# Gram inputs in 4 KB rows, own PSUM banks for the first Gram blocks, VectorE copying part of them, and raw weights queued directly behind the first loads

## The chip, the cores and the metric

The kernel runs on one core of a Trainium2 chip. The metric is the device time of one execution in microseconds (us); lower is better. The core has a matrix engine (TensorE, PE in the profile, with PEld for its weight loads), VectorE (DVE), ScalarE (ACT), GpSimd (POOL) and SyncE (SP), whose instruction stream issues all DMA transfers of this kernel.

## What is computed

A delta-rule attention runs over 768 steps for 4 x 8 heads of width 48; its output, 3072 tokens of 384 features, passes through two dense layers with a hidden width of 2048 each.

```
k_n = k / (norm(k) + 1e-6)
for t in range(S):
    y[:, :, t] = einsum('bhd,bhde->bhe', q[:, :, t], state)
    v_old = einsum('bhde,bhd->bhe', state, k_n[:, :, t])
    state += beta[t] * einsum('bhd,bhe->bhde', k_n[:, :, t], v[:, :, t] - v_old)
x  = y as (3072, 384)
x1 = elu(x @ w_in) @ w_out
h  = x1 @ w_in2
g  = (a0 + a1 h + a2 h^2 + a3 h^3) / (1 + |b0| |h| + |b1| h^2 + 1e-6)
out = g @ w_out2
```

## The kernel before, in words

**Attention.** The 768 steps are cut into 12 sub-chunks `s` of 64 steps, and two sub-chunks make one of six windows `w` (512 tokens over the four batches). For each sub-chunk, `g_item` builds Gram blocks (k times [k, q]) in two steps, `bb` = 0 and 1, of 64 small matmuls each into two PSUM tiles (`gp`, one for each `hf`). From each tile VectorE writes the masked k-q part to `p`; ScalarE copies two 32-column diagonal pieces to `gd` and one off-diagonal piece to `lo`. When the four Gram steps of a window are done, VectorE turns `gd` over into `am` (`pre1`) and works through a triangular inverse of about 60 dependent small operations (`row`, `merge`), whose last step turns the result into `tp_t` (`post`). Then `chain` runs the sub-chunks one after the other: solve (`cb`), lower part (`lo`), second solve, outputs (`y`, turned over as `xt`), state update (`ku` into `s_bd`), and for s > 0 the product with the state (`ks`).

**Dense layers.** For each window the first layer takes 16 steps `H` (hidden block `h`) and `O` (output block `o`), each nine matmuls of 128x512. The second layer follows for six groups of 512 tokens. Operands are split in a high and a low part. The weights come as 8-byte numbers: `conv_load` brings a 192 KB piece into one of eight slots inside the tile `wo1` (shown as `wo` in the trace), and `conv_x` (two ScalarE operations), `conv_d` (VectorE: three or two SCALAR_TENSOR_TENSOR operations of 128x192 a piece, written to `wo` and `ce`) and `conv_s` turn it into the high and low part, `wi` for the first matrix.

**Order.** Every operation is first recorded by `Recorder` with the dependencies that its tiles make. `order` then lays out the five engines' streams from these dependencies and from tables of durations and switching costs (`PEC`, `LEAVE`, `PAIR`, `SLACK`), with pseudo-random tie-breaks from the seeds in `MIX`. Two engines that read one PSUM tile are put one behind the other in the order in which the program names them. Before the first wide matmul, `gaps` puts `fill` matmuls (128x256, no result used) into planned idle time of TensorE; each runs as two passes in the trace.

**Around the change.** Gram inputs are loaded by `gin_ahead`, once for each sub-chunk and `bb`: two transfers of 48 partitions (rows 0 to 47 and 64 to 111), each with two 2 KB pieces a partition. The first six tiles are parked in buffers that are not needed yet (`wo1`, then `xs`, `xh`, `xl`; the trace shows `wo` and `xg`); later ones use two rotating buffers `gin`, and each Gram step frees its tile and asks for the next. Gram PSUM tiles come from the pool `pa` of three banks. `start` issues the first loads; `chain_loads` follows with `kq`, `kv` and the first eight pieces of raw weights.

Of the kernel before, what the change touches and what calls it, by code (L numbers as in the profile page):

```python
# [20 lines left out]
D = 48  # L21
# [8 lines left out]
HD = DM // 2  # L30
NV = 7
Q = dict(
# [142 lines left out]
class Recorder:  # L175
    def __init__(self, nc):
        self.nc, self.ops, self.group, self.live = nc, [], None, False

# [80 lines left out]
    def dma(self, out, in_):  # L259
        v = out if isinstance(out, View) else in_  # L260
        n = v.ids.size * 4 * (v.part[1] - v.part[0])
        self.add("SP", self.nc.sync.dma_start, dict(out=out, in_=in_), [out], [in_], SLACK["issue"], 2000, n)

# [45 lines left out]
LEAVE = {"F": 2040, "so": 774, "lo": 812, "ks": 960, "gp": 970, "ku": 855, "yy": 1471, "xx": 290, "wm": 500, "yt": 1400}  # L309
ENTER = {"F": 0, "so": 71, "ks": 71, "xx": -25, "ku": 70, "yy": 20, "gp": 60, "lo": 100, "wm": 50, "yt": 20}  # L310
PAIR = {
# [3 lines left out]
SIZE = {"F": 9, "yy": 16, "yt": 48}  # L315
SLACK = {"small": 150, "F": 100, "x": 30, "issue": 560, "rate": 240, "land": 2300, "wait": 1500, "space": 3900, "room": 290, "first": 432, "hold": 400, "jit": 300, "pj": 0}
MIX = [
    (1076044, 1), (92414181, 200), (90150106, 200), (77610261, 20), (97147800, 60), (84287398, 200),
    (75730493, 60), (8425654, 600),
]  # L320
# [241 lines left out]
def kernel(  # L562
# [172 lines left out]
    gin_t = {}  # L735
    gin_q = [(w, j, s, bb) for w in range(NW) for j, s in enumerate(WINS[w]) for bb in range(2)]
    gin_n = [0]
# [11 lines left out]
    def gin_ahead(n):  # L749
        for _ in range(n):  # L750
            i = gin_n[0]
            if i == len(gin_q):
                return
            park = i < 6
            if park or gin_l[0] < 2:
                w, j, s, bb = gin_q[i]
# [5 lines left out]
                t = t.rearrange("p (f n) -> p f n", f=2)  # L762
# [36 lines left out]
    def g_item(j, s, bb):  # L799
# [6 lines left out]
        t, n = gin_t.pop((s, bb))  # L806
        for i in range(4):
            for blk in range(2):
                for hf in range(2):
                    for h in range(2):  # L810
                        rows, c = slice(64 * h, 64 * h + D), 128 * i
                        mm(out=ps[hf][grp(hf, h, blk), i], lhsT=t[rows, hf, c + 32 * blk:c + 32 * blk + 32], rhs=t[rows, hf, c:c + 128],
                           start=True, stop=True)
        gin_l[0] -= n
        gin_ahead(1)
        for hf in range(2):
            u0, v0 = 16 * j + 8 * hf + 4 * bb, 8 * hf + 4 * bb
            vector.tensor_tensor(
                out=p_t[:, v0:v0 + 4], in0=ps[hf][:, :, 64:128],
                in1=mp_sb[hf].unsqueeze(1).to_broadcast([128, 4, 64]), op=ALU.mult)  # L820
            b0, b1 = halves(hf)
            act(out=gd[b0, u0:u0 + 4], in_=ps[hf][b0, :, 0:32], func=AF.Copy)
            act(out=gd[b1, u0:u0 + 4], in_=ps[hf][b1, :, 32:64], func=AF.Copy)
            act(out=lo_t[b0, 4 * bb:4 * bb + 4], in_=ps[hf][b0, :, 32:64], func=AF.Copy)
# [513 lines left out]
    def start():  # L1338
        gpsimd.memset(gd, 0.0)
        gpsimd.memset(s_bd, 0.0)  # L1340
        gin_ahead(1)
        rc.dma(out=cm_sb, in_=mask_p)
        gin_ahead(NV)
        load_beta(0)
        rc.dma(out=mh_sb, in_=mask_h)

    def chain_loads():
        for nm in ("kq", "kv"):
            for _ in range(2 if nm == "kq" else 2):
                ch_ahead(nm)  # L1350
        conv_ahead()

    def coefs():
# [204 lines left out]
```

## Time and profile before

| | |
|---|---|
| median of 3 runs | 1002.14 us (1002.08 to 1002.99) |
| the profiled execution | 1002.51 us, of which the span of its instructions is 1000.7 us |
| TensorE / VectorE / ScalarE / GpSimd busy | 98% / 85% / 75% / 38% of the span |
| DMA | 96.77 MB, mean 97 GB/s |

A span starts with the first instruction and ends with the last; 1.81 us of the profiled execution lie outside it. The share of busy time is a mean over stages that have different limits, so the stages are shown apart below.

### The profile page before, as it was taken

To read this page: it belongs to the slowest core of one execution; us is meant where nothing else is said; L and a number is where in the kernel's file an instruction comes from. 1 tells how busy PE (TensorE), PEld (TensorE's weight loads), DVE (VectorE), ACT (ScalarE), POOL (GpSimd) and SP (SyncE) were. 2 spreads that over 40 slices of the span, in tenths; PEclk is the share of its full clock that TensorE was granted. 3 is DMA by queue.
4 is the path that set the end of the run, shared out by engine and by line. 5 is a ranking of instruction groups with operands and counts; after the bars stand their busy time and mean duration, and the time that the engine had idled before them with its cause. 6 is when DMAs were issued, how large, how long until landed. Compare 5 with 4: busy or idle time off the path is not lost.

```text
span 1000.7 us, 25423 instructions
## 1 busy us (share of the span) xinstructions
PE 982.7 (98%) x10402; PEld 801.3 (80%) x10402; DVE 846.6 (85%) x1218; ACT 753.1 (75%) x1524; POOL 382.5 (38%) x282
## 2 busy tenths in 40 slices
PE   6999999999999999999999999999999999999997
PEld 4877878877887887788888888888888888888885
DVE  3999969987995998799666477889999999999996
ACT  3779799887877887887788778676676676766763
POOL 2353546542331242223222244364363643633332
PEclk9999999999999999999999999999999999999998
DMA  9554074226426432641545932001010010000000
GB/s 236 141 166 156 20 216 140 64 82 209 139 66 184 146 115 77 183 139 64 163 121 187 357 125 79 1 23 42 0 64 1 1 64 1 32 1 0 32 1 31
DMA packets 61588, 96.77 MB, mean 97 GB/s; under 512 B 7072, under 2 KB 39968, under 8 KB 61472
## 3 DMA queue, kind: packets, MB, share of 16 engines
q1 hardware_dynamic: 61472, 95.15, 30.4%
q8 instruction: 81, 1.33, 0.6%
q14 instruction: 35, 0.29, 0.1%
HBM read 73.11 MB, written 22.02 MB: 95 GB/s over the span
## 4 chain that ended last, share of the span: by engine, by line
PE 95%; DVE 2%; ACT 1%; issue 1%; DMA 0%; SPq 0%; ACTq 0%; DVEq 0%
PE o L193 39%; PE h L193 19%; PE h_b L193 10%; PE h_a L193 9%; PE fill L1478 4%; PE cb L193 3%; PE y L193 3%; PE gp L193 3%; PE ku L193 1%; PE ks L193 1%; PE h_c L193 1%; PE xt L193 1%; ACT wo L193 1%; DVE wo L193 1%; DMA wo<-c_kq 0%
## 5 line engine op out<-in xcount | busy, mean ns | idle before, releaser
L193 POOL TENSOR_TENSOR wor<-wo,wor 128x384 fp32r<-128x384 f32 x96 | 114.9, 1199 | 283.9 <-ACT wor L193 260.3
L193 POOL TENSOR_TENSOR gl<-wo 128x1024 fp32r<-128x1024 f32 x47 | 138.8, 2953 | 189.1 <-DVE wo L193 142.8
L193 PE MATMUL o<-gh,wor 128*128 128x512 f32 x576 | 195.1, 396 | 0.0
L193 PE MATMUL h<-xh,wi 128*128 128x512 f32 x546 | 185.5, 398 | 0.0
L193 ACT ACTIVATE wo<-wo 128x1024 f32<-128x1024 f32 (+3 forms) x224 | 142.3, 672 | 41.9 <-DVE wo L193 37.8
L193 PE MATMUL o<-gh,wo 128*128 128x512 f32 x576 | 139.7, 391 | 0.0
L193 PEld LDWEIGHTS o<-gh,wor 128*128 128x128 f32 x576 | 108.1, 188 | 23.9 <-issue 0.2
L193 PEld LDWEIGHTS o<-gh,wo 128*128 128x128 f32 x576 | 108.9, 189 | 22.7
L193 PEld LDWEIGHTS h<-xh,wi 128*128 128x128 f32 x546 | 102.4, 188 | 23.1 <-issue 0.6
L193 PE MATMUL o<-gl,wor 128*128 128x512 f32 x288 | 112.2, 390 | 0.0
L193 PE MATMUL h<-xl,wi 128*128 128x512 f32 x273 | 106.4, 390 | 0.3 <-DVE xl L193 0.3
L193 DVE SCALAR_TENSOR_TENSOR e<-e,pe 128x512 f32<-128x512 f32 x96 | 74.4, 775 | 37.4 <-ACT e L193 36.6
L193 DVE SCALAR_TENSOR_TENSOR wo<-wo 128x192 int32<-128x192 int32 (+2 forms) x101 | 87.4, 869 | 17.9 <-ACT wo L193 17.6
L193 PE MATMUL h_b<-xh,wi 128*128 128x512 f32 x300 | 96.4, 389 | 0.0
L193 DVE TENSOR_TENSOR gl<-e,gh 128x512 fp32r<-128x512 f32 x88 | 74.1, 843 | 20.2 <-ACT gh L193 19.9
L193 PE MATMUL h_a<-xh,wi 128*128 128x512 f32 x276 | 88.9, 389 | 0.0
L193 ACT ACTIVATE wo<-h_b,ab_sb 128x1024 f32<-128x1024 f32 (+1 forms) x52 | 57.3, 1128 | 33.5 <-PE h_b L193 33.5
L193 PE MATMUL o<-gl,wo 128*128 128x512 f32 x288 | 73.8, 391 | 2.0 <-DVE gl L193 2.0
L193 ACT ACTIVATE e<-h 128x512 f32<-128x512 f32 x91 | 54.4, 597 | 27.1 <-PE h L193 25.8
L193 DVE SCALAR_TENSOR_TENSOR gh<-wo,ab_sb 128x1024 fp32r<-128x1024 f32 (+1 forms) x49 | 63.3, 1293 | 7.5 <-ACT wo L193 1.7
L193 ACT ACTIVATE wo<-h_a,ab_sb 128x1024 f32<-128x1024 f32 x46 | 52.0, 1161 | 21.2 <-PE h_a L193 19.7
L193 ACT ACTIVATE wor<-wo 128x384 fp32r<-128x384 f32 x96 | 50.3, 524 | 21.6 <-PE o L193 19.6
(125 smaller groups left out, 2037.8 us busy)
## 6 DMA issues: line engine op xcount, KB each, us to landing
kq<-c_kq SPq DMA_DIRECT2D x22, 512.0 KB, 4.5
kv<-c_kv SPq DMA_DIRECT2D x24, 384.0 KB, 4.7
raw<-w_out SPq DMA_DIRECT2D x42, 192.0 KB, 2.7
gin<-c_kq SPq DMA_DIRECT2D x36, 192.0 KB, 3.8
raw<-w_in SPq DMA_DIRECT2D x34, 192.0 KB, 2.9
o2d<-cs SPq DMA_DIRECT2D x32, 192.0 KB, 2.5
i2d<-cs SPq DMA_DIRECT2D x32, 192.0 KB, 2.7
wi<-i2d SPq DMA_DIRECT2D x16, 384.0 KB, 3.3
```

Source lines behind the costliest of these rows:

```text
L193: fn(**{k: v.real() if isinstance(v, View) else v for k, v in kw.items()})
L1478: nc.tensor.matmul(out=wt["w"][:, 0:256], lhsT=c[:, 128:256], rhs=c, start=True, stop=True)
```

## The change

Gram inputs are loaded once for each sub-chunk and `hf`, 112 partitions of one 4 KB row in a single transfer (448 KB, with the 16 empty rows between the two blocks of 48); both tiles of a sub-chunk serve both Gram steps and come free after the second. The second Gram step of all uses the two PSUM tiles of the first dense layer (`h0`, `h1`), the third two of its output tiles (`o1`, `o2`). In the first window VectorE copies the `gd` pieces of `hf` = 1. Eight pieces of raw weights are queued behind the fourth Gram load, and all later transfers are put behind them until `chain_loads` has been recorded. The planner's tables and seeds change too.

```
-    wm1=6, wk=4, wr=3, wr0=4)
+    wm1=6, wk=4, wr=3, wr0=4, wl=8, gh=1)
...
+        if v.ids.size >= 1024:
+            n *= .75
+        o = self.add("SP", self.nc.sync.dma_start, dict(out=out, in_=in_), [out], [in_], SLACK["issue"], 2000, n)
+        if self.behind is not None:
+            o.deps.setdefault(self.behind, "s")
+        self.sent = o
...
-    "F": (226.7, 425), "gp": (27.3, 475), "ks": (13.4, 330), "so": (22, 220), "lo": (22, 250), "yy": (85, 262), "ku": (47, 263),
+    "F": (226.7, 425), "gp": (29, 475), "ks": (18, 330), "so": (22, 220), "lo": (22, 250), "yy": (85, 262), "ku": (47, 263),
...
-                for h in range(2):
-                    rows = slice(64 * h, 64 * h + D)
-                    rc.dma(out=t[rows], in_=c_kq[s, :, rows, 4 * bb:4 * bb + 4, :].rearrange("f p u n -> p f (u n)"))
-                gin_t[s, bb] = t, not park
+                t = t.rearrange("p (u n) -> p u n", u=8)
+                rc.dma(out=t[0:64 + D], in_=c_kq[s, hf, 0:64 + D])
+                gin_t[s, hf] = t, not park
...
-        ps = [pa.tile([128, 4, 128], F32, tag="pa", name="gp") for _ in range(2)]
+        i = 2 * s + bb
+        if i == 1:
+            ps = h_s
+        elif i == 2:
+            ps = [po.tile([128, 512], F32, tag=t, name="gp") for t in ("o1", "o2")]
+        else:
+            ps = [pa.tile([128, 512], F32, tag="pa", name="gp") for _ in range(2)]
...
-        gin_l[0] -= n
-        gin_ahead(1)
+        if bb:
+            for hf in range(2):
+                gin_l[0] -= gin_t.pop((s, hf))[1]
+            gin_ahead(2)
...
+            if j == s and hf == Q["gh"]:
+                vector.tensor_copy(out=gd[b0, u0:u0 + 4], in_=ps[hf][b0, :, 0:32])
+                vector.tensor_copy(out=gd[b1, u0:u0 + 4], in_=ps[hf][b1, :, 32:64])
+            else:
+                act(out=gd[b0, u0:u0 + 4], in_=ps[hf][b0, :, 0:32], func=AF.Copy)
+                act(out=gd[b1, u0:u0 + 4], in_=ps[hf][b1, :, 32:64], func=AF.Copy)
...
-        gin_ahead(NV)
+        gin_ahead(3)
         load_beta(0)
+        conv_loads(Q["wl"])
+        rc.behind = rc.sent
         rc.dma(out=mh_sb, in_=mask_h)
+        for _ in range(2):
+            ch_ahead("kv")
+        gin_ahead(4)
```

What the tables do to the streams shows in the streams themselves. In the rows a name before the arrow is written and the names behind it are read; `x8` counts equal rows.

SyncE's stream from the program's start, before (`wo_86` is the tile `wo1`, `bl` is beta, `cm_sb` the masks, `mh_sb` a small mask):

```order
1 L193 DMA wo_86<-c_kq 48x2x512 x2
2 L193 DMA cm_sb<-mask_p 128x256
3 L193 DMA wo_86<-c_kq 48x2x512 x4
4 L193 DMA xg<-c_kq 48x2x512 x2
5 L193 DMA bl<-beta_l 128x32
6 L193 DMA xg<-c_kq 48x2x512 x4
7 L193 DMA gin<-c_kq 48x2x512 x4
8 L193 DMA kv<-c_kv 128x768 x2
9 L193 DMA mh_sb<-mask_h 128x2
10 L193 DMA kq<-c_kq 128x1024 x2
11 L193 DMA wo_86<-w_in 128x384 x8
```

The same place of the stream with the change:

```order
1 L192 DMA wo_86<-c_kq 112x1024 x2
2 L192 DMA xg<-c_kq 112x1024
3 L192 DMA wo_86<-c_kq 112x1024
4 L192 DMA cm_sb<-mask_p 128x256
5 L192 DMA bl<-beta_l 128x32
6 L192 DMA wo_86<-w_in 128x384 x8
7 L192 DMA xg<-c_kq 112x1024 x2
8 L192 DMA gin<-c_kq 112x1024 x2
9 L192 DMA kv<-c_kv 128x768 x2
10 L192 DMA mh_sb<-mask_h 128x2
11 L192 DMA kq<-c_kq 128x1024 x2
12 L192 DMA raw<-w_out 128x384 x2
```

The raw weights move from behind sixteen Gram transfers, `kv` and `kq` to behind the four Gram transfers of the first window; the masks move from the third place to the fifth.

VectorE's stream at the program's start, before (the Gram blocks of the first window, the turn into `am`, and the first steps of the inverse):

```order
1 L193 TENSOR_TENSOR p<-gp,cm_sb 128x256 x8
2 L193 STREAM_TRANSPOSE am<-gd 128x1024
3 L193 TENSOR_TENSOR p<-gp,cm_sb 128x256
4 L193 TENSOR_SCALAR x<-am 128x32
5 L193 TENSOR_TENSOR p<-gp,cm_sb 128x256
6 L193 TENSOR_TENSOR nb<-rr,x 128x32
```

And with the change, from the third Gram step on (rows with `wo_86` and `ce` are weight conversions):

```order
6 L192 TENSOR_TENSOR p<-gp,cm_sb 128x256
7 L192 COPY gd<-gp 64x128 x2
8 L192 TENSOR_TENSOR p<-gp,cm_sb 128x256
9 L192 SCALAR_TENSOR_TENSOR wo_86<-wo_86 128x192
10 L192 TENSOR_TENSOR p<-gp,cm_sb 128x256
11 L192 COPY gd<-gp 64x128 x2
12 L192 TENSOR_TENSOR p<-gp,cm_sb 128x256
13 L192 STREAM_TRANSPOSE am<-gd 128x1024
14 L192 SCALAR_TENSOR_TENSOR wo_86<-wo_86 128x192
15 L192 TENSOR_SCALAR x<-am 128x32
16 L192 SCALAR_TENSOR_TENSOR ce<-wo_86 128x192 x2
17 L192 SCALAR_TENSOR_TENSOR wo_86<-wo_86 128x192 x2
```

Eight copies stand ahead of the turn, and conversions begin there. From the turn into `am` to the turn into `tp_t` the stream holds 22 conversions before and 35 with the change; from there to the first subtraction for the dense layer (`xl`) 30 and 28.

SyncE's stream beside the second window's dense layer, before:

```order
47 L193 DMA raw<-w_in 128x384 x2
48 L193 DMA gin<-c_kq 48x2x512 x2
49 L193 DMA kq<-c_kq 128x1024
50 L193 DMA wo_86<-w_out 128x384 x2
51 L193 DMA gin<-c_kq 48x2x512 x2
```

And with the change:

```order
45 L192 DMA raw<-w_out 128x384 x2
46 L192 DMA gin<-c_kq 112x1024 x2
47 L192 DMA kq<-c_kq 128x1024
48 L192 DMA wo_86<-w_in 128x384 x2
49 L192 DMA kv<-c_kv 128x768
```

The two Gram transfers there now bring the whole next sub-chunk into the two buffers that the step before has just freed. TensorE's stream has two groups of nine wide matmuls between that step and the next one, where it had one.

## Rows read from the trace of the kernel before

**Rows 1.** The page's first part: busy time, share of span and instructions of each engine.

```profile
PE 982.7 (98%) x10402; PEld 801.3 (80%) x10402; DVE 846.6 (85%) x1218; ACT 753.1 (75%) x1524; POOL 382.5 (38%) x282
```

**Rows 2.** Engines' busy time in four stretches; then granted clock, DMA share, GB/s.

```profile
0.00:19.05 19.05, 9.79 (x260) 6.61 (x260) 3.03 (x9) 6.69 (x24) 3.84 (x7) 1.00 0.96 187
19.05:57.40 38.35, 38.11 (x398) 32.26 (x398) 35.45 (x78) 26.28 (x97) 14.83 (x18) 1.00 0.58 181
57.40:88.10 30.70, 28.96 (x855) 22.80 (x853) 28.25 (x77) 25.93 (x83) 14.09 (x22) 1.00 0.60 187
88.10:1000.70 912.60, 905.79 (x8897) 739.59 (x8892) 779.86 (x1057) 694.24 (x1322) 349.73 (x235) 1.00 0.28 88
```

**Rows 3.** Waits of TensorE from 88 us on: total us, times, longest.

```profile
PE o L193 <- DVE gl L193: 2.0, 1, 2.0
PE h L193 <- DVE xl L193: 0.3, 1, 0.3
```

**Rows 4.** Timeline of TensorE: start, duration, operation, count, wait before it.

```profile
4.75 1.96 PE L193 MATMUL gp<-wo 48*32 48x128 f32 x62 [0.34 <-DMA wo<-c_kq]
23.87 1.34 PE L193 MATMUL gp<-xg 48*32 48x128 f32 x64
...
30.07 1.16 PE L193 MATMUL gp<-gin 48*32 48x128 f32 x64
31.16 26.60 PE L1478 MATMUL fill<-cm_sb 128*128 128x256 f32 x122
...
88.09 0.50 PE L193 MATMUL h<-xh,wi 128*128 128x512 f32 x1
```

**Rows 5.** Timeline of VectorE: first and last Gram masks, and the turns.

```profile
6.76 0.76 DVE L193 TENSOR_TENSOR p<-gp,cm_sb 128x256 f32<-128x256 f32 x2 [6.76 <-PE gp L193]
...
17.48 0.76 DVE L193 TENSOR_TENSOR p<-gp,cm_sb 128x256 f32<-128x256 f32 x2 [3.31 <-PE gp L193]
19.05 1.96 DVE L193 STREAM_TRANSPOSE am<-gd 128x1024 f32<-128x1024 f32 x1 [0.81 <-ACT gd L193]
...
55.36 2.02 DVE L193 STREAM_TRANSPOSE tp_t<-am 128x1024 f32<-128x1024 f32 x1
```

**Rows 6.** DMA, 0.5 to 1 us: transfer, count, size, us to landing.

```profile
wo<-c_kq SPq DMA_DIRECT2D x1, 192.0 KB, 3.0
```

**Rows 7.** DMA totals from 4 to 18 us, then from 19 to 27 us.

```profile
DMA packets 1743, 2.83 MB, mean 202 GB/s; under 512 B 373, under 2 KB 397, under 8 KB 1742
...
DMA packets 1741, 3.11 MB, mean 389 GB/s; under 512 B 342, under 2 KB 1304, under 8 KB 1739
```

**Rows 8.** Instruction groups up to 90 us: count, busy us, mean ns, idle before.

```profile
L193 ACT ACTIVATE gd<-gp 64x128 f32<-64x128 f32 x32 | 8.5, 269 | 15.2 <-DVE p L193 14.6 <-DVE x L193 0.3
L193 ACT ACTIVATE wo<-wo 128x192 int32<-128x192 uint32 x37 | 13.8, 381 | 0.3 <-DMA wo<-w_out 0.2
L193 DVE TENSOR_TENSOR p<-gp,cm_sb 128x256 f32<-128x256 f32 x16 | 6.4, 420 | 17.1 <-PE gp L193 17.1
L193 DVE COPY s_bd<-ku 48x384 f32<-48x384 f32 x4 | 2.1, 551 | 0.0
```

**Rows 9.** Instruction groups of VectorE from 19.05 to 57.4 us.

```profile
L193 DVE SCALAR_TENSOR_TENSOR wo<-wo 128x192 int32<-128x192 int32 x14 | 5.8, 417 | 0.0
L193 DVE SCALAR_TENSOR_TENSOR ce<-wo 128x192 int32<-128x192 int32 x9 | 3.6, 396 | 0.2 <-POOL wi L193 0.2
```

**Rows 10.** VectorE's waits from 19.05 to 57.4 us.

```profile
DVE p L193 <- PE gp L193: 1.9, 3, 1.1
DVE nb L193 <- ACT rr L193: 0.4, 1, 0.4
```

**Rows 11.** One instruction group of VectorE from 57.4 to 88.1 us.

```profile
L193 DVE TENSOR_TENSOR tmp<-tt,am 128x1024 f32<-128x1024 f32 x1 | 1.2, 1227 | 0.0
```

**Rows 12.** Timeline of TensorE at two Gram steps inside the dense layer.

```profile
126.19 1.16 PE L193 MATMUL gp<-gin 48*32 48x128 f32 x64
...
131.01 1.16 PE L193 MATMUL gp<-gin 48*32 48x128 f32 x64
```

**Rows 13.** Landing of transfers of 512 KB, 163.5 to 166 us, then 135 to 137 us.

```profile
kq<-c_kq SPq DMA_DIRECT2D x2, 512.0 KB, 4.2
...
kq<-c_kq SPq DMA_DIRECT2D x1, 512.0 KB, 5.7
```

More of the change, by code (lines that the diff above doesn't have):

```diff
@@ L30 @@
 HD = DM // 2
-NV = 7
 Q = dict(
@@ L176, in __init__ @@
     def __init__(self, nc):
-        self.nc, self.ops, self.group, self.live = nc, [], None, False
+        self.nc, self.ops, self.group, self.live, self.behind, self.sent = nc, [], None, False, None, None
     def brk(self, kind):
@@ L261, in dma @@
         n = v.ids.size * 4 * (v.part[1] - v.part[0])
-        self.add("SP", self.nc.sync.dma_start, dict(out=out, in_=in_), [out], [in_], SLACK["issue"], 2000, n)
+        if v.ids.size >= 1024:
[4 more added lines that the diff above has]
+        self.sent = o
     class Eng:
@@ L306 @@
 PEC = {
[L307 removed]
+    "F": (226.7, 425), "gp": (29, 475), "ks": (18, 330), "so": (22, 220), "lo": (22, 250), "yy": (85, 262), "ku": (47, 263),
     "xx": (90, 405), "wm": (200, 500), "yt": (33, 260)}
[L309 removed]
+LEAVE = {"F": 2040, "so": 774, "lo": 812, "ks": 1307, "gp": 1086, "ku": 855, "yy": 1471, "xx": 290, "wm": 500, "yt": 1400}
 ENTER = {"F": 0, "so": 71, "ks": 71, "xx": -25, "ku": 70, "yy": 20, "gp": 60, "lo": 100, "wm": 50, "yt": 20}
 PAIR = {
[1 row of a table removed]
[1 row of a table added]
     ("F", "ku"): 2230, ("F", "yt"): 2266, ("yy", "yy"): 1371, ("yy", "ku"): 1371, ("yy", "xx"): 1421, ("yy", "gp"): 1500,
@@ L315 @@
 SIZE = {"F": 9, "yy": 16, "yt": 48}
-SLACK = {"small": 150, "F": 100, "x": 30, "issue": 560, "rate": 240, "land": 2300, "wait": 1500, "space": 3900, "room": 290, "first": 432, "hold": 400, "jit": 300, "pj": 0}
+SLACK = {"small": 150, "F": 100, "x": 30, "issue": 560, "rate": 290, "land": 2300, "wait": 1500, "space": 3900, "room": 290, "first": 432, "hold": 400, "jit": 300, "pj": 0}
 MIX = [
-    (1076044, 1), (92414181, 200), (90150106, 200), (77610261, 20), (97147800, 60), (84287398, 200),
-    (75730493, 60), (8425654, 600),
+    (1076044, 1), (90150106, 200), (77610261, 20), (84287398, 200), (75730493, 60), (8425654, 600),
+    (40729345, 60), (28945668, 20), (17928448, 20),
 ]
@@ L735 @@
     gin_t = {}
-    gin_q = [(w, j, s, bb) for w in range(NW) for j, s in enumerate(WINS[w]) for bb in range(2)]
+    gin_q = [(w, s, hf) for w in range(NW) for s in WINS[w] for hf in range(2)]
     gin_n = [0]
@@ L755, in gin_ahead @@
             if park or gin_l[0] < 2:
-                w, j, s, bb = gin_q[i]
+                w, s, hf = gin_q[i]
                 if park:
@@ L803, in g_item @@
         p_t, lo_t = p_d[s], lo_d[s]
-        ps = [pa.tile([128, 4, 128], F32, tag="pa", name="gp") for _ in range(2)]
+        i = 2 * s + bb
[5 more added lines that the diff above has]
+            ps = [pa.tile([128, 512], F32, tag="pa", name="gp") for _ in range(2)]
+        ps = [t.rearrange("p (u n) -> p u n", u=4) for t in ps]
         rc.brk("gp")
-        t, n = gin_t.pop((s, bb))
-        for i in range(4):
+        ts = [gin_t[s, hf][0] for hf in range(2)]
+        for u in range(4 * bb, 4 * bb + 4):
             for blk in range(2):
@@ L810, in g_item @@
                     for h in range(2):
-                        rows, c = slice(64 * h, 64 * h + D), 128 * i
-                        mm(out=ps[hf][grp(hf, h, blk), i], lhsT=t[rows, hf, c + 32 * blk:c + 32 * blk + 32], rhs=t[rows, hf, c:c + 128],
+                        rows = slice(64 * h, 64 * h + D)
+                        mm(out=ps[hf][grp(hf, h, blk), u % 4], lhsT=ts[hf][rows, u, 32 * blk:32 * blk + 32], rhs=ts[hf][rows, u],
                            start=True, stop=True)
-        gin_l[0] -= n
-        gin_ahead(1)
+        if bb:
+            for hf in range(2):
+                gin_l[0] -= gin_t.pop((s, hf))[1]
+            gin_ahead(2)
         for hf in range(2):
@@ L1342, in start @@
         rc.dma(out=cm_sb, in_=mask_p)
-        gin_ahead(NV)
+        gin_ahead(3)
         load_beta(0)
+        conv_loads(Q["wl"])
+        rc.behind = rc.sent
         rc.dma(out=mh_sb, in_=mask_h)
+        for _ in range(2):
+            ch_ahead("kv")
+        gin_ahead(4)
     def chain_loads():
-        for nm in ("kq", "kv"):
-            for _ in range(2 if nm == "kq" else 2):
-                ch_ahead(nm)
+        for _ in range(2):
+            ch_ahead("kq")
         conv_ahead()
+        rc.behind = None
     def coefs():
```

3 lines of the change are left out of this document (removed), and 2 rows, old and new, of the table PAIR.

## The prediction

> **What bounds the kernel now.** I read the page's totals first, then the stretches, then the waits of the engine that is busiest, then the start instruction by instruction. TensorE is busy for 98% of the span [rows 1]. [...] Before 88.1 us TensorE looks busy too, but one row alone, 122 passes of fill, is 26.6 us of it [rows 4]: it waits. The engine with the work there is VectorE: 35.45 of 38.35 us from the turn into `am` to the first solve and 28.25 of 30.7 us from there to the wide matmuls, but only 3.03 of the first 19.05 us [rows 2]. [...] The change touches the 19.05 us, adds to the work, and gives the later Gram steps another supply.
>
> **1. First loads and Gram steps.** Before, the four Gram steps of the first window are masked from 6.76 to 18.2 us, and VectorE's wait ahead of the last was 3.31 us for TensorE [rows 5]. They ran one after another through transfers, matmuls and the freeing of three banks. The start of this is latency: the first 192 KB landed 3.0 us after issue at 0.74 us [rows 6]. The rate decides the rest. From 4 to 18 us, where Gram pieces of 48 partitions filled the queue, DMA moved 202 GB/s; from 19 to 27 us, with `kq` and raw weights over 128 partitions, 389 [rows 7]. A transfer of 112 partitions isn't in the trace; these two are its bounds. I take 389, because `kq` shares its source, its 4 KB rows and nearly all its partitions, and the slow ones share only the source.
>
> [...]
>
> At 389 GB/s a load of 0.459 MB takes 1.18 us: the four land at about 4.4, 5.6, 6.8 and 8.0 us, the masks at 8.3 (3.2 us of issue and latency ahead of the first). Gram step one runs from 5.6 us for 2.0 us [rows 4], the others follow, each in its own banks, in 1.3 to 1.9 us: the fourth ends near 12.1. VectorE can mask from 8.3 us: four steps with two masks at 0.34 us apart (two in 0.76 [rows 5]) and two copies, for which the nearest rows are ScalarE's 0.27 and VectorE's 0.55 for three times the columns [rows 8]; I take 0.25, bounds 0.15 and 0.42. That is 1.2 us a step, 4.8 in all, ending at 13.3. ScalarE has 14 pieces at 0.25 and four conversions at 0.38 [rows 8] ahead of the last `gd`, 5.0 us from 8.6 on, ending at 13.6. The turn starts at **13.8 us instead of 19.05**. At 202 GB/s the masks land at 12.5, and the turn starts at 17.8.
>
> **2. VectorE from the turn to `tp_t`.** Before it took from 19.05 to 57.38 us, 38.3 us [rows 5]. The stream now holds 13 conversions more there. One is busy 0.40 to 0.42 us [rows 9], of which some 0.07 overlaps the next; 0.27 to 0.42 each, I take 0.34: +4.4 us (3.5 to 5.4). The waits of 1.9 us for Gram matmuls and 0.4 for ScalarE's square root [rows 10] now have conversions or earlier data in them: −2.0 (0 to −2.3). So 40.7 us (39.5 to 43.8), and `tp_t` is ready at 54.5 us, 2.9 earlier.
>
> **3. The fill ahead of the first solve.** TensorE has its own condition, as fills are plain instructions in its stream: 67 now instead of 61, that is 134 passes at 0.218 us (26.60/122 [rows 4]), 29.2 us, behind the last Gram step of the second window. That step needs the banks of the one before, whose mask stands 30 instructions behind the turn: 11 conversions and 5 masks at 0.34 and 14 small ones at about 0.2 give 8.2 us after 15.7; then three ScalarE pieces (0.8 us) and the matmuls (1.2): 25.9 us. The solve can't start before 55.1 us. This, not `tp_t`, comes last by a little. Before, fill and `tp_t` ended together at 57.7 [rows 4, 5]. Gain so far: **2.6 us**.
>
> ScalarE's stream has a raw `w_out` piece ahead of those three pieces. In the queue 3.67 MB of Gram and 3.75 MB of other data (masks, eight raw pieces, `kv`, `kq`, itself) come ahead of its landing: at 389 GB/s 2.7 + 19.1 = 21.8 us, hidden behind VectorE's 23.9.
>
> **4. From the solve to the wide matmuls.** Two conversions fewer (−0.7) and one 128x1024 product (1.2 us [rows 11]) that now stands behind `xl`. VectorE was busy 28.25 of 30.7 us there [rows 2], so part of it counts: −1.0 (0 to −1.9). The wide matmuls start 3.6 us earlier, at 84.5.
>
> **5. After that.** TensorE's stream has the same 3456 wide matmuls, cut into 68 runs instead of 69, and the same small groups; the clock was at its upper level throughout [rows 2]. Nil, ±0.5, if nothing waits. The one new wait: both Gram tiles of the next sub-chunk are requested only when the second step of this one has ended. Before, from one Gram step to the next was 4.82 us with one group of nine wide matmuls between [rows 12]; now two groups stand there, 2.04 us more, so 5.70 us pass from the end of the first to the start of the next. A load of 512 KB lands 4.2 us after issue, 5.7 at worst in the rows I read [rows 13]; the second is issued some 0.45 us later. Typical 4.2 + 0.45 + 0.1 plus up to 1 us of the second's own bytes: 4.8 to 5.7 us. It just fits, and I count 0. It comes four times. Queued behind these two on SyncE are `kq` and `kv` for the chain and raw weights, which have an `H` group or more to spare.
>
> **The sum.** 2.6 + 1.0 = 3.6 us off the profiled 1002.51 us is 998.9. The median of the runs is 0.37 us below the profiled one, so for the median I forecast 1002.14 − 3.6 = **998.5 us**, with its own range 996.5 to 1000.1.
>
> **Rivals.**
>
> *Slow Gram transfers* (slower). If 112 partitions move at 202 GB/s, the turn is only 1.25 us earlier, and the raw piece in ScalarE's stream lands at 2.7 + 18.2 + 9.6 = 30.5 us. The three Gram pieces behind it wait, then the last Gram step, then 29.2 us of fill: the first solve starts at 61.7 instead of 57.7. With the 1.0 us of step 4 this is +3.0, 1005.1 us. It turns from gain to loss below about 241 GB/s (raw piece landing at 27.5 us). For it: SyncE's early transfers have never been fast in this trace. Against it: 389 GB/s as soon as the partitions were many [rows 7].
>
> *No cover for the loads inside the dense layer* (slower from a point on). If each pair takes the 5.7 us of [rows 13] plus 0.45 plus the second's 1.2, it is 7.4 us against 5.70: 1.7 us of waiting TensorE, four times, +6.8, giving 1005.3 us. From 0.9 us each it cancels the gain; slower beyond 0.2% needs 1.4 us each. For it: the transfers there share the queue with raw weights. Against it: 4.2 us is the common landing, and TensorE waited for no transfer there before [rows 3]. [...]
>
> *The gain is eaten on VectorE* (no change). If the conversions cost 0.42 us each, the waits stay and the turn comes at 14.5 (copies at 0.42), `tp_t` is ready at 14.5 + 38.3 + 5.4 = 58.2 us, 0.8 later than before, and with step 4 the time is 1002. The raw weights that are done earlier buy nothing later, as TensorE doesn't wait for them there. For it: VectorE is 92% busy in this stretch [rows 2]. Against it: 16 of the first 19 us are idle on VectorE.
>
> **How the numbers follow.** About 0.2%, 2.0 us, can be told from no change here. Forecast 0.65 (faster), gain eaten 0.17 (no change), slow transfers 0.09 and uncovered loads 0.09 (slower where they come in full, no change where in part: 0.04 of the two). The forecast's upper end spills little over 1000.1, and a partly eaten gain can still be over 2.0 us: faster 0.66, same 0.20, slower 0.14. The range reaches down to 995.8, where steps 2 and 4 are at their better bounds, and up to 1003.8, which takes in the eaten gain and the partial cases of the two others.
>
> **What would show it.** Right: the first masks near 8.3 us and the turn into `am` at 13 to 14.5 us; DMA above 330 GB/s in the first 12 us; 35 conversions between the turns and `tp_t` near 54.5; the first solve directly behind the fill; the first wide matmul at 83.5 to 85.5 us; no wait of TensorE for `gin` behind it. Wrong: a turn after 17 us, ScalarE idle ahead of a `raw` piece at 23 to 30 us, TensorE rows with a wait for a `c_kq` transfer after 85 us, or wide matmuls that start at 88 us with an earlier turn.

## The result: 1.2% slower, and the profile after

The changed kernel takes 1014.4 us (median of 4 runs, 1012.76 to 1015.79) against 1002.11 beside it: 1.0122 times as long, 95% interval [1.0104, 1.0141]. The forecast was 998.5 us, with a range up to 1003.8; it was wrong in sign. The profile after is of the fastest of the four runs.

First the page's totals of the changed kernel, which answer to [rows 1]:

```profile
PE 983.8 (97%) x10400; PEld 802.1 (79%) x10400; DVE 855.3 (85%) x1226; ACT 754.2 (75%) x1516; POOL 386.7 (38%) x282
```

The same four stretches as in [rows 2], cut at its own turn, first solve and first wide matmul (columns: stretch, length, busy us of PE, PEld, DVE, ACT, POOL, granted clock, DMA share, GB/s):

```profile
0.00:15.99 15.99, 7.45 (x256) 6.40 (x256) 5.49 (x17) 6.41 (x20) 3.84 (x7) 0.99 0.91 283
15.99:63.98 47.99, 40.87 (x405) 33.78 (x406) 40.98 (x93) 33.62 (x121) 19.79 (x27) 0.86 0.57 176
63.98:93.56 29.58, 27.48 (x849) 21.79 (x849) 27.97 (x74) 23.80 (x75) 14.34 (x21) 1.00 0.52 160
93.56:1011.00 917.44, 907.97 (x8899) 740.09 (x8892) 780.89 (x1045) 690.38 (x1301) 348.72 (x227) 1.00 0.27 88
```

The totals tell little: the largest difference is VectorE's, 855.3 us for 846.6. The stretches tell more. The first is 3.1 us shorter than before (15.99 for 19.05), the second 9.6 longer (47.99 for 38.35), the third 1.1 shorter, the fourth 4.8 longer (917.44 for 912.60). So the loss is in two places: 5.5 us ahead of the first wide matmul (93.56 for 88.09 us) and 4.8 behind it. Together they are 10.3 us, the difference of the two profiled spans; the medians are 12.3 us apart, as the executions of either kernel scatter by 2 to 3 us.

VectorE up to `tp_t`, to be read against [rows 5] and [rows 10]: its timeline, the masks with waits and the turns only (start, duration, operation, and in brackets the wait ahead of it).

```profile
9.70 0.76 DVE L192 TENSOR_TENSOR p<-gp,cm_sb 128x256 f32<-128x256 f32 x2 [0.54 <-DMA cm_sb<-mask_p]
...
14.70 0.43 DVE L192 TENSOR_TENSOR p<-gp,cm_sb 128x256 f32<-128x256 f32 x1 [1.14 <-PE gp L192]
...
15.99 1.96 DVE L192 STREAM_TRANSPOSE am<-gd 128x1024 f32<-128x1024 f32 x1
21.00 0.42 DVE L192 TENSOR_TENSOR p<-gp,cm_sb 128x256 f32<-128x256 f32 x1 [1.13 <-PE gp L192]
...
27.07 0.42 DVE L192 TENSOR_TENSOR p<-gp,cm_sb 128x256 f32<-128x256 f32 x1 [3.81 <-PE gp L192]
...
30.95 0.42 DVE L192 TENSOR_TENSOR p<-gp,cm_sb 128x256 f32<-128x256 f32 x1 [1.67 <-PE gp L192]
...
61.74 1.98 DVE L192 STREAM_TRANSPOSE tp_t<-am 128x1024 f32<-128x1024 f32 x1
```

From the turn to the end of `tp_t` are 47.7 us, 38.3 before. Behind the turn three masks wait 6.6 us for Gram matmuls, 1.9 before [rows 10]. The conversions of raw weights in this stretch, which answer to [rows 9] (count, busy us, mean ns):

```profile
L192 DVE SCALAR_TENSOR_TENSOR wo<-wo 128x192 int32<-128x192 int32 x22 | 10.7, 492 | 0.1
L192 DVE SCALAR_TENSOR_TENSOR ce<-wo 128x192 int32<-128x192 int32 x14 | 5.5, 400 | 0.0
```

16.2 us for 36 of them, 9.4 for 23 before: 6.8 more. Why the masks wait is on TensorE, in its timeline of the second window's Gram steps (answers to [rows 4]):

```profile
17.44 0.64 PE L192 MATMUL gp<-xg 48*32 48x128 f32 x4 [2.76 <-DMA xg<-c_kq]
19.02 1.96 PE L192 MATMUL gp<-xg 48*32 48x128 f32 x64 [0.94 <-ACT rr L192]
22.35 1.08 PE L192 MATMUL gp<-xg 48*32 48x128 f32 x25 [1.37 <-DVE t L192]
25.86 1.49 PE L192 MATMUL gp<-xg 48*32 48x128 f32 x35 [2.44 <-issue]
...
33.86 29.19 PE L1498 MATMUL fill<-cm_sb 128*128 128x256 f32 x134
63.98 0.20 PE L192 MATMUL cb<-kv,tp_t 32*32 32x48 f32 x1 [0.93 <-DVE wo L192]
```

The fifth step waits for its transfer, which the raw weights now stand ahead of; the sixth stands still for 2.44 us in its middle for nothing that the profile shows ("issue"). The last Gram step ends at 33.86 us, the fill of 29.19 us behind it at 63.05, and the solve starts at 63.98 (57.7 before). Between the two it waits 0.93 us for VectorE, whose `tp_t` ends at 63.72: VectorE comes last here, by 0.7 us.

Last, TensorE's waits from the first wide matmul on, where [rows 3] had the end's 2.0 us and 0.3:

```profile
PE o L192 <- DVE gl L192: 2.1, 1, 2.1
PE o L192 <- POOL gl L192: 1.0, 1, 1.0
PE gp L192 <- DMA gin<-c_kq: 0.8, 2, 0.7
PE gp L192 <- DVE cs L192: 0.5, 1, 0.5
PE o L192 <- DVE gh L192: 0.3, 1, 0.3
PE h L192 <- DVE xl L192: 0.2, 1, 0.2
```

Beside the end's 2.1 us these are five small waits, 2.8 us, against 0.3 before; the wait for `gin` that a rival spoke of is 0.8 us of them. The matmuls themselves are 2.2 us longer (907.97 for 905.79).

### The profile page after: what moved, and what is told of

Read it like the earlier page. It is cut to its first block, busy times and chain, and to the rows that moved or that the text cites. A ratio compares the mean times of both kernels' runs of the same rounds, so it can differ in the third digit from the quotient of the medians.

```text
span 1011.0 us, 25373 instructions
## 1 busy us (share of the span) xinstructions
PE 983.8 (97%) x10400; PEld 802.1 (79%) x10400; DVE 855.3 (85%) x1226; ACT 754.2 (75%) x1516; POOL 386.7 (38%) x282
## 3 DMA queue, kind: packets, MB, share of 16 engines
q1 hardware_dynamic: 59168, 96.72, 29.6%
## 4 chain that ended last, share of the span: by engine, by line
PE 88%; DVE 5%; DMA 2%; issue 2%; ACT 1%; POOL 1%; ACTq 0%; SPq 0%; DVEq 0%; POOLq 0%
PE o L192 37%; PE h L192 18%; PE h_b L192 10%; PE h_a L192 9%; PE gp L192 3%; PE cb L192 3%; PE y L192 3%; PE ku L192 1%; DVE wo L192 1%; PE ks L192 1%; DMA gin<-c_kq 1%; DVE tmp L192 1%; PE h_c L192 1%; PE xt L192 1%; ACT wo L192 1%
## 5 line engine op out<-in xcount | busy, mean ns | idle before, releaser
L192 DVE SCALAR_TENSOR_TENSOR e<-e,pe 128x512 f32<-128x512 f32 x96 | 77.1, 803 | 58.5 <-ACT e L192 57.8
L192 DVE SCALAR_TENSOR_TENSOR wo<-wo 128x192 int32<-128x192 int32 (+2 forms) x101 | 94.5, 941 | 12.8 <-ACT wo L192 12.5
L192 ACT ACTIVATE gh<-e 128x512 fp32r<-128x512 f32 x96 | 60.4, 630 | 10.2 <-DVE e L192 4.7
```

The source lines that it names most:

```text
L192: fn(**{k: v.real() if isinstance(v, View) else v for k, v in kw.items()})
```

## The experiments

Two ways of making a version were used, and their difference turned out to be the finding. A *planned* version edits the source and lets the planner order all streams again. A *laid-over* version records the operations of before, so that the planner gives the streams of before, word for word, and only then changes what single operations emit, or moves named ones. All ratios are to the kernel before, run beside the version on the same chip, with 95% intervals. "Wide" is the start of the first wide matmul in the profiled execution, "rest" the span behind it.

### Planned versions: parts of the change undone or alone

**The old order of loads**, all else changed:

```diff
-        gin_ahead(3)
+        gin_ahead(7)
         load_beta(0)
-        conv_loads(Q["wl"])
-        rc.behind = rc.sent
         rc.dma(out=mh_sb, in_=mask_h)
...
```

> The changed kernel with the first loads in the old order: masks second, all eight Gram tiles (4 KB rows) ahead of kv, kq and the raw weights. Theory 'weights first' (the raw weights in front make the Gram loads of the second window and TensorE's instruction fetches late, VectorE stands in order at their masks): the first wide matmul is at 85 to 88 us instead of 93.6 and the time falls by 5 to 8 us, to 1006 to 1009. Theory 'tables' (the new planning tables and seeds give a worse stream): no change beyond 2 us, 1012 to 1016. Theory 'uncovered loads' (two buffers emptied together): no change either.

1012.06 us, 1.0108 [1.0081, 1.0134]; wide 91.99, rest 917.0. Without the early raw weights the kernel is still 10.4 us above before, where the whole change is 12.3, and the intervals overlap. "Weights first" (1006 to 1009 us, wide at 85 to 88) did not come.

**The old planner tables**, all else changed:

```diff
-    "F": (226.7, 425), "gp": (29, 475), "ks": (18, 330),
+    "F": (226.7, 425), "gp": (27.3, 475), "ks": (13.4, 330),
...
-    (1076044, 1), (90150106, 200), (77610261, 20), (84287398, 200),
+    (1076044, 1), (92414181, 200), (90150106, 200), (77610261, 20),
...
```

> The changed kernel planned with the old tables, transfer rates and seeds. Theory 'tables': 1001 to 1005 us. Theory 'weights first': the loads keep their order, so the first wide matmul stays at 92 to 95 us, 1011 to 1017 us.

1011.45, 1.0093 [1.0075, 1.0112]; wide 93.25, rest 918.0. The new tables aren't it either.

**The 4 KB rows alone**, on the kernel before:

```diff
-                for h in range(2):
-                    rows = slice(64 * h, 64 * h + D)
-                    rc.dma(out=t[rows], in_=c_kq[s, :, rows, 4 * bb:4 * bb + 4, :].rearrange("f p u n -> p f (u n)"))
+                rc.dma(out=t[0:64 + D], in_=c_kq[s, hf, 0:64 + D])
...
```

> The kernel before with the 4 KB Gram rows alone (both tiles of a sub-chunk freed after its second Gram step; old start order, banks, ScalarE copies and tables). Theory 'weights first': about as before, 1000 to 1004 us, as the weights stay behind. Theory 'uncovered loads': waits of TensorE for gin of 1 us and more at each second sub-chunk of a window, 1006 to 1010 us (the old tables expect shorter loads, so there is no second group of wide matmuls ahead of the step).

1014.07, 1.0123 [1.0108, 1.0138]; wide 92.41, rest 919.8. That is above what either theory gave, and TensorE has no wait for `gin` behind the first wide matmul, so "uncovered loads" is not the reason. One part alone cost as much as the whole, and taking away another part left the loss nearly as it was: a sum of parts does not explain this.

**4 KB rows only in the first three sub-chunks**, the rest of the change kept (loads inside the dense layer as before, two for each half step):

```diff
+                if park:
                     rc.dma(out=t[0:64 + D], in_=c_kq[s, hf, 0:64 + D])
+                else:
+                    for h in range(2):
+                        rows = slice(64 * h, 64 * h + D)
+                        rc.dma(out=t[rows], in_=c_kq[s, :, rows, 4 * hf:4 * hf + 4, :].rearrange("f p u n -> p f (u n)"))
...
```

> The changed kernel with 4 KB rows for the first three sub-chunks alone; from the fourth on the old loads by half steps, freed and reloaded after each Gram step. Theory 'uncovered loads': no TensorE wait for gin after 100 us and 4 to 6 us less, 1008 to 1011. Theory 'weights first': at most 2 us less, 1012 to 1015, with the first wide matmul at 92 us or later.

1011.83, 1.0105 [1.0086, 1.0123]; wide 93.72, rest 913.5. TensorE no longer waits for `gin`; the kernel is still 10.2 us above before.

### Planned versions: nothing but the planner's draw

The planner breaks ties by a hash of a first seed, and lets further seeds replace it for one operation in 20, 60, 200 or 600 (`MIX`). So the order can be drawn anew with no edit to loads, banks or copies.

**Before, with the first seed alone**, and **before, with another single seed** (5550123 in place of 1076044):

```diff
-MIX = [
-    (1076044, 1), (92414181, 200), (90150106, 200), (77610261, 20), (97147800, 60), (84287398, 200),
-    (75730493, 60), (8425654, 600),
-]
+MIX = [(1076044, 1)]
```

> The kernel before with all but the first of the planner's seeds taken out: same loads, banks, copies and tables, only ties fall otherwise. Theory 'fitted stream' (the stream before is one lucky draw of many, and any new plan lies some 10 us above it): 1007 to 1014 us. Theory 'the loads are to blame' (rows, weights first): 1000 to 1004 us.

> The kernel before planned with one other seed in place of all of its own: a second draw. Theory 'fitted stream': 1006 to 1014 us, as in the first draw (1010.7). Theory 'the first draw was a bad one': 1000 to 1005 us.

1010.66, 1.0079 [1.0064, 1.0094], wide 90.84, rest 917.0; and 1010.33, 1.0075 [1.0055, 1.0094], wide 89.84, rest 920.4. The four longest of TensorE's waits behind 90 us in the first of them:

```profile
PE o L193 <- DVE gl L193: 2.1, 1, 2.1
PE h_c L193 <- ACT pe L193: 1.2, 1, 1.2
PE gp L193 <- issue: 0.9, 1, 0.9
PE o L193 <- DVE gh L193: 0.9, 1, 0.9
```

These are small scattered waits like those of the changed kernel, at other places, in a kernel whose loads, banks and copies are those of before.

**Before, with the change's tables and seeds** (the second diff above, the other way round):

> The kernel before planned with the new tables, transfer rates and seeds, nothing else changed. Theory 'fitted stream': 1007 to 1014 us, as the seeds were chosen for other loads. Theory 'the loads are to blame': 1000 to 1005 us.

1008.1, 1.0060 [1.0038, 1.0083]; wide 90.50, rest 914.7. The seeds that the change brings do not suit the kernel before.

**The change, with the first seed alone**:

> The changed kernel with all but the first seed taken out. Theory 'fitted stream': its seeds are no fit either, so another draw lies within 5 us of 1014.4 on either side, 1009 to 1019. Theory 'the tables belong to the change': worse by 5 us and more, 1019 or over.

1011.27, 1.0095 [1.0077, 1.0112]; wide 94.26, rest 914.2. At the same single seed before stands at 1.0079 and the change at 1.0095, with overlapping intervals. So on an order drawn without the further seeds the change makes no difference that these runs tell; the order of before is worth 0.75 to 0.79%, about 8 us. The seeds that the change brings gain it nothing either: 1.0122 with them, 1.0095 without, with intervals that just overlap.

**The change's streams, with the second window's Gram loads put ahead of six of the eight raw weights** (no new draw, one move in SyncE's stream):

```diff
...
+    late = [o for o in first if o in raw_o[2:8]]
+    first = [o for o in first if o not in late]
+    i = max(first.index(o) for o in gin_o[4:8]) + 1
+    first = first[:i] + late + first[i:]
```

> The changed kernel with its streams as they are, but the second window's four Gram transfers moved in SyncE's stream ahead of the last six of the eight raw weight transfers. Theory 'weights first': the fifth Gram step starts 2.5 to 4 us earlier (at 14 to 16.5 instead of 19.0 us), VectorE's wait of 3.8 us behind it shrinks, the first wide matmul moves from 93.6 to 89 to 91 us, 1010 to 1012 us. Theory 'fitted stream' alone: no change beyond 1.5 us.

1011.47, 1.0100 [1.0085, 1.0115], which overlaps the changed kernel's interval; wide 93.63, rest 918.1. The head is as long as ever, but not for the same reasons. TensorE's fourth Gram step, VectorE's turn, and VectorE's waits for Gram matmuls from the turn to the end of `tp_t`:

```profile
16.05 0.31 PE L192 MATMUL gp<-xg 48*32 48x128 f32 x1 [3.13 <-issue]
...
18.42 1.97 DVE L192 STREAM_TRANSPOSE am<-gd 128x1024 f32<-128x1024 f32 x1
...
DVE p L192 <- PE gp L192: 2.3, 2, 1.6
```

The fifth step (at 18.35 us) no longer waited for its transfer, the mask waits shrank from 6.6 us to 2.3, and turn to `tp_t` took 45.05 us instead of 47.73. But the fourth step stood still for 3.13 us instead of 1.44, the turn came 2.4 us later, and `tp_t` ended at 63.47 (63.72 in the changed kernel). So moving the weights alone does not shorten the head; that their place costs nothing is not shown, as one delay took the other's place. TensorE's clock is low here all the same:

```profile
16.00:20.00 4.00, 3.04 (x101) 2.43 (x101) 2.83 (x5) 1.17 (x5) 0.00 (x0) 0.52 1.05 338
20.00:24.00 4.00, 0.32 (x16) 0.00 (x0) 3.15 (x11) 3.99 (x18) 1.46 (x3) 0.50 0.87 274
```

### Laid-over versions: the streams of before, word for word

**Each Gram load as one transfer of 112 partitions** in place of two of 48 (`alt` is what the first of the two emits; the second emits nothing):

```diff
...
-                    rc.dma(out=t[rows], in_=c_kq[s, :, rows, 4 * bb:4 * bb + 4, :].rearrange("f p u n -> p f (u n)"))
+                    both = slice(0, 64 + D)
+                    rc.dma(out=t[rows], in_=c_kq[s, :, rows, 4 * bb:4 * bb + 4, :].rearrange("f p u n -> p f (u n)"),
+                           alt=() if h else (t[both], c_kq[s, :, both, 4 * bb:4 * bb + 4, :].rearrange("f p u n -> p f (u n)")))
```

> The kernel before with all five engines' streams word for word as they were, but each pair of 48-partition Gram transfers sent as one transfer of 112 partitions (pieces of 2 KB). Theory 'fitted stream': nothing is replanned, so no loss, 997 to 1002 us, with the turn into am 1 to 3 us earlier and over 300 GB/s in the first 14 us. Theory 'the loads are to blame': as far as it lies in the 112 partitions, a loss of several us.

1001.57, 0.9990 [0.9981, 1.0000]; wide 87.74, rest 911.3. The turn came at 18.67 us, only 0.4 earlier. The DMA totals from 4 to 14 us, where Gram loads of 112 partitions filled the queue:

```profile
DMA packets 1675, 2.93 MB, mean 293 GB/s; under 512 B 251, under 2 KB 270, under 8 KB 1674
```

That is about midway between the 202 and 389 GB/s of [rows 7].

**The eight raw weight transfers behind the fourth Gram load**, two transfers of 48 for each load:

```diff
...
+    early = raw_o[0:8]
+    first = [o for o in first if o not in early]
+    i = first.index(gin_o[3]) + 1
+    first = first[:i] + early + first[i:]
```

> The kernel before with the same streams, but the eight first raw weight transfers moved in SyncE's stream to right behind the first window's Gram transfers. Theory 'weights first': the second window's Gram loads land 4 to 5 us later, the last Gram step and the fill behind it move with them, first wide matmul at 91 to 93 us, 1004 to 1007 us. Theory 'fitted stream': nothing but SyncE's stream is changed, 1000 to 1004 us.

1002.96, 1.0005 [0.9991, 1.0018]; wide 90.67, rest 912.2. No loss that these runs tell.

**One transfer for each load, and own PSUM banks for Gram steps 2 and 3**:

```diff
...
+            if 2 * s + bb == 1:
+                v.base.other = lambda k=k: h_s[k].base.get().rearrange("p (u n) -> p u n", u=4)
+            elif 2 * s + bb == 2:
+                v.base.other = lambda k=k: po.real.tile([128, 512], F32, tag=f"o{k + 1}", name="gp").rearrange("p (u n) -> p u n", u=4)
```

> The kernel before with its streams as they were, the Gram pairs sent as one transfer of 112 partitions, and the second and third Gram step in the PSUM tiles that the change gives them. Theory 'fitted stream': two parts of the change without a new plan gain, the turn into am at 14.5 to 16.5 us instead of 19.05 and the time 997 to 1001. Theory 'the loads and banks are to blame': 1005 or more.

1000.0, 0.9979 [0.9969, 0.9989]; turn at 17.39 (14.5 to 16.5 was expected), wide 88.31, rest 910.5. The first version whose whole interval lies below 1.

**Those two and VectorE's copies**:

```diff
...
+                if j == s and hf == 1:
+                    def emit(o_=o_, i_=i_):
+                        nc.vector.tensor_copy(out=o_.real(), in_=i_.real())
...
```

> One transfer for each Gram load, own PSUM banks and the VectorE copies on the streams of before; the raw weights stay where before has them. If the copies on VectorE shorten the way to the turn into am, as the prediction's step 1 has it, 999 to 1000 us with the turn before 17.4 us, where the same kernel without the copies has it; if they hold VectorE up, as rival 'gain eaten on VectorE' has it, 1001 to 1003 us.

999.15, 0.9974 [0.9964, 0.9983]; turn at 17.10, wide 88.34, rest 911.4. The lowest time of all, 0.26% below before, and so below the changed kernel. Against the version without the copies the intervals overlap, so the copies' own share is not shown. TensorE's first Gram steps in it:

```profile
5.00 1.96 PE L195 MATMUL gp<-wo 48*32 48x128 f32 x64 [5.00 <-DMA wo<-c_kq]
6.94 1.96 PE L195 MATMUL h<-wo 48*32 48x128 f32 x64
9.25 1.97 PE L195 MATMUL gp<-wo 48*32 48x128 f32 x64 [0.34 <-DMA wo<-c_kq]
10.97 1.20 PE L195 MATMUL gp<-xg 48*32 48x128 f32 x31
14.56 1.49 PE L195 MATMUL gp<-xg 48*32 48x128 f32 x37 [2.40 <-issue]
```

The steps follow one another as the prediction's step 1 had it, up to a stop of 2.40 us in the middle of the fourth that the profile puts down to nothing.

**Three versions with raw weights early over banks and copies**: banks and weights; also the copies; also the 4 KB rows in the first three sub-chunks.

> As g4_banks_raw_dve, with ScalarE making all block copies as in before: one transfer for each Gram load, own PSUM banks, raw weights early, on the streams of before. Sum of the two runs that did each alone (-2.1 us for transfers and banks together, +0.8 us for the raw weights): 1000.8. Theory 'fitted stream': 999 to 1003. Rival 'the edits cost': the raw weights fill the queues that the earlier Gram steps now need: 1004 or more.

> As g5_whole, with the 2 KB rows of before in every Gram load. Theory 'fitted stream': 998.5 to 1004. Rival 'the edits cost': within 1 us of g5_whole if the rows are not what costs, 3 us or more below it if they are.

> The instruction streams of before, word for word, with the whole change laid over them by hand for the part of the program ahead of the dense layer: every Gram load one 112-partition transfer, 4 KB rows in the first three sub-chunks, Gram steps 2 and 3 in PSUM banks of their own, the half of the first window's blocks copied by VectorE, and the eight raw weight transfers right behind the fourth Gram transfer. Nothing is planned anew. Theory 'fitted stream' (the loss comes from planning the streams again, not from the edits): within 1002 +/- 3.5 us, 998.5 to 1005.5, no more than 0.3% above before. Rival 'the edits cost' (the VectorE copies, the rows and the early raw weights lengthen the head whatever the stream): first wide matmul at 92 to 94 us as in after, against 88.1 in before, and 1006 us or more.

1004.37, 1.0026 [1.0017, 1.0034]; 1004.63, 1.0024 [1.0016, 1.0033]; 1006.09, 1.0045 [1.0033, 1.0057]. By their text the first and the third would have spoken for "the edits cost", and the second fits neither theory. But in all three the weights went behind the first Gram load and not behind the fourth, and a Gram step then waited for its transfer (5.4 us in the first of the three). They price a misplaced burst of weights (wide at 91 to 94 us, rest 911.8 to 912.4), not the change.

**The whole change up to the dense layer, weights in their place**, and **the same without the early weights** (the diff is the first one's, against the third version above):

```diff
...
-                    gin_o.append(rc.ops[-1])
+                    if not h:
+                        gin_o.append(rc.ops[-1])
...
```

> As g5_whole, with the eight raw weight transfers where the change has them, behind the fourth Gram load (in g5_whole, g4_banks_raw_dve and g3_banks_raw they stood behind the first Gram load, three loads too early, and the second Gram step waited 5.4 us for its transfer). The whole change up to the dense layer, on the streams of before. Theory 'fitted stream': 999 to 1004 us, so that 8 us or more of the 12 lost are the replanned streams. Rival 'the edits cost': 1005 to 1008 us, as g5_whole had it (1006.1), so that a third to a half of the loss is the edits'.

> g6_banks_dve with 4 KB rows in the first three sub-chunks; the raw weights stay late, as before has them. Against g6_banks_dve (999.15) it prices the rows, against h1_whole the early raw weights. Theory 'fitted stream': 998.5 to 1001, rows worth nothing on fixed streams or up to 1.5 us (the difference between g5_whole and g4_banks_raw_dve), because a sub-chunk's first step now needs two loads in place of one. Rival 'the edits cost': 1002 or more.

1002.15, 1.0004 [0.9992, 1.0016], wide 88.97, rest 910.6; and 1001.92, 0.9995 [0.9987, 1.0004], wide 89.92, rest 910.7. The second lies between the ranges of its two theories. The first decides most of it: with one-transfer loads, 4 KB rows, own banks, VectorE's copies and early weights all in, on the streams of before, the time is that of before. Its stretch of the dense layer:

```profile
88.97:999.60 910.63, 904.16 (x8900) 738.46 (x8892) 780.48 (x1055) 693.73 (x1321) 349.31 (x235) 1.00 0.28 89
```

TensorE's only wait in it:

```profile
PE o L195 <- DVE gl L195: 2.0, 1, 2.0
```

And VectorE's waits in it from the turn (16.84 us) to the end of `tp_t` (58.16); L850 is where this version emits the Gram matmuls on 4 KB rows:

```profile
DVE p L195 <- PE gp L850: 3.9, 2, 2.2
DVE p L195 <- PE gp L195: 1.1, 1, 1.1
DVE nb L195 <- ACT rr L195: 0.4, 1, 0.4
```

The turn is 2.2 us earlier than before and `tp_t` 0.8 later: 5.0 us of waiting for Gram matmuls have taken the place of 1.9. The prices by pairs: the rows cost about 0.2% (0.9974 [0.9964, 0.9983] without them, 0.9995 [0.9987, 1.0004] with; the intervals don't touch), the early weights nothing that can be told (0.9995 and 1.0004). With the rows and late weights the turn is at 19.96 us and not at 17.10. A sub-chunk's first Gram step now needs two loads where it needed one, and TensorE's "issue" stop is 4.1 us long and not 2.4; how much of the 2.9 us is either was not separated. With the same rows and early weights the stop is 2.12 us and the turn at 16.84, so the rows alone do not set the turn.

Side by side, the rest of the span behind the first wide matmul: 910.5 to 912.4 us in the nine laid-over versions (912.6 in before), 913.5 to 920.4 in the ten with an order planned anew, the change among them, each from one profiled execution. The two groups don't overlap. TensorE's busy time in it follows: 904.0 to 905.8 us laid over, 906.7 to 908.7 in the three draws of before without an edit to loads, banks or copies, 908.0 in the changed kernel.

The start of the first wide matmul divides otherwise: 88.09 in before, 89.84 to 90.84 us in the three draws without an edit, 91.99 to 94.26 in the seven planned versions that hold the change or a part of it. So a new draw alone accounts for 1.8 to 2.8 of the 5.5 us lost ahead of the dense layer; the rest comes only where edit and new order meet, as the edits on the old streams, with the weights in their place, start it at 87.74 to 90.67.

## Why the prediction was wrong

The profiled run was forecast at 998.9 us and took 1012.76, 13.9 more: 9.1 ahead of the first wide matmul (93.56 for 84.5) and 4.8 behind it. Steps 2 and 3 failed on the first part, largely by one and the same delay, and step 5 on the second. Nowhere was the new order of the streams itself given a price.

**Step 1 (first loads and Gram steps): right in direction, 2.2 us short.** From 4 to 8 us, with only Gram loads at the head of the queue, 294 GB/s moved, midway between the bounds and not at the upper one (389) that was taken; the 359 and 329 of the next two stretches hold raw weights too. At 294 GB/s the prediction's own sum puts the masks at 9.9 us (an estimate); they landed at 9.7 instead of 8.3. The fourth Gram step then stood still for 1.44 us, and the turn came at 15.99 us, not 13.8. (At the lower bound the same sum gives the masks at 12.9, not the 12.5 of the prediction; nothing hangs on it.)

**Step 2 (VectorE from the turn to `tp_t`): failed.** Forecast 40.7 us, measured 47.7. Thirteen conversions more was right, but the conversions took 6.8 us more and not 4.4. The waits were to shrink by 2.0 us; they grew by 4.3 (6.6 for 1.9 and 0.4). The prediction moved the masks earlier and never asked whether the Gram steps behind them, 5 to 8, could follow: the loads of the fifth and sixth step stand behind eight raw weights, and the first of them was waited for until 17.4 us. This term fails on the old streams too (5.0 us of waiting for 1.9). The version with the Gram loads ahead has 2.3 us of it left, but a later turn. What else makes steps 5 to 8 late (the "issue" stop of 2.44 us, the granted clock of 0.50, the order of small pieces on three engines) was not separated.

**Step 3 (the fill ahead of the first solve): the fill was right, the path to it wrong.** The fill lasts 29.19 us (forecast 29.2). But the Gram step ahead of it was to end at 25.9, paced by VectorE's masks, and ended at 33.86: the fifth and sixth step ended at 20.98 and 27.35, and the last two follow them with fills between and no wait shown. The masks waited for Gram steps (6.6 us) far longer than the steps shown waited for VectorE (1.37 us), so the path ran through TensorE's steps. Nor does the fill come last, as was said: 33.86 + 29.19 = 63.05, `tp_t` is ready at 63.72, and the solve starts behind that, 8.9 us after the 55.1 of the prediction.

**Step 4 (from the solve to the wide matmuls): right in size,** 29.6 us for 30.4, −0.8 where −1.0 was forecast; its two terms were not measured apart.

**Step 5 (after that): failed.** "Nil, ±0.5" was argued from the same number of wide matmuls, runs and small groups. It is +4.8 us. The mechanism looked for (loads that no longer fit between two Gram steps) is there, with 0.8 us. The rest goes with the order: the streams behind 90 us are a new draw of the planner, and each new draw in these runs costs 1 to 8 us there against 912.6, the three without any edit 2 to 8. The prediction read the order where the edit was and took the rest for equivalent because it was made of the same pieces. In before, TensorE waits for 2.3 us in 912 [rows 3]; that is a property of one order, not of the work.

**The rivals.** "Slow Gram transfers" fell: 294 GB/s is above the 241 at which it would have turned to a loss. "No cover" is there in small. "The gain is eaten on VectorE" named the right place, but with a loss of 0.8 us in `tp_t`; in the planned kernel it is 6.3. That the whole change on the old streams shows 0.8 too is luck: that version has no more conversions there, only a turn 2.2 us earlier and 3.1 us more of waiting for Gram matmuls. No rival held that the new order itself is worse, though the diff replaced the planner's seeds; this was the case that decided.

**How much is what.** Of the 12.3 us, the edits ahead of the dense layer bring none on the old streams (1.0004 [0.9992, 1.0016]). Two draws without any edit cost 0.75 and 0.79%, about 8 us, a third, with the change's tables, 0.60%. The remaining 4 us or so are not assigned: a worse draw, or the edits in the head of a new order. Not tried on the old streams: the 4 KB rows inside the dense layer, and the raw weights' conversions brought forward, both of which come only with a new plan. What makes the order of before good was not found, only that the other orders tried are worse.

## What to carry to other kernels

When a change passes through a planner, measure the planner's own scatter first: draw the order anew with no edit, and lay the edit over the old order. Here the scatter was 6 to 8 us, always to the worse, and the edit laid over the old order, with its parts in their places, between −2.8 and +0.6 us. And when a wait in front of a stage is shortened, follow the next stage's inputs as well: the 3 us gained at the turn were lost again to waits for Gram steps, the first of which had its loads behind other traffic, and to conversions.

## What the runs showed of the hardware

**The clock in a sparse head.** Stretches of 4 us of the changed kernel (columns as in the second fence; the last is the GB/s of step 1):

```profile
4.00:8.00 4.00, 2.21 (x68) 1.75 (x72) 0.00 (x0) 0.00 (x0) 0.37 (x1) 1.00 1.02 294
8.00:12.00 4.00, 4.00 (x163) 4.00 (x153) 2.73 (x9) 1.68 (x7) 0.00 (x0) 1.00 1.08 359
12.00:16.00 4.00, 1.25 (x55) 0.65 (x39) 2.78 (x10) 3.44 (x13) 0.00 (x0) 0.96 1.02 329
16.00:20.00 4.00, 1.62 (x44) 1.23 (x52) 3.87 (x9) 3.81 (x17) 1.08 (x3) 0.50 1.03 284
20.00:24.00 4.00, 2.06 (x65) 1.14 (x49) 2.25 (x11) 2.88 (x12) 0.92 (x2) 0.50 1.04 363
24.00:28.00 4.00, 2.14 (x37) 1.62 (x38) 0.94 (x4) 0.47 (x3) 2.16 (x4) 0.50 0.86 318
```

TensorE was busy 1.25 of 4 us from 12 us on, and for the 12 us from 16 on the granted clock was 0.50; before, it was 1.00 in each of the four stretches of [rows 2]. A stretch as sparse was not always followed by a low clock: in the version with one-transfer loads and own banks TensorE was busy 1.36 of the 4 us from 12 us on, and the granted clock was 1.00 in every 4 us from 4 to 32. Nor does the low clock alone decide the time: one of the four runs of the changed kernel had a mean clock of 0.999, with a span of 1012.1 us beside 1011.0 at 0.991, and the whole change on the old streams has such a stretch too (0.50 from 16 to 20 us) and is as fast as before.

**Stops without a releaser.** In the middle of an early Gram step TensorE stood still, for nothing that the profile shows: in the changed kernel for 1.44 us up to 13.95 us and for 2.44 up to 25.86. Thirteen versions have Gram steps with banks of their own, the changed kernel among them. In ten of these the longest such stop seen in the first 30 us is 2.1 to 4.1 us; in the other three (the old order of loads, the old tables, the 4 KB rows only in the first three sub-chunks) the longest of the whole span is 3.8, 1.0 and 1.6 us. Of the seven versions without such banks, before has one stop there, of 0.56 us. The one-transfer loads alone, the first seed alone and the moved raw weights (these from 10 us on) show none there, the 4 KB rows alone show none in the whole span, and for the two others it was not shown. Why is open. The profile lists packets of instructions among the DMA queues (116 in the changed kernel, 1.62 MB): one in the 2.44 us of the changed kernel's longer stop, none in the 1.44 us of the shorter. That TensorE's instructions came late is a guess; no run took the traffic away.
